# Block attention with decay followed by a two-layer network: the opening list laid out anew, decays spread by TensorE, zero fills in four, half products for w_in's second quarter

## The chip, the cores and the metric

The kernel runs on one core of one Trainium2 chip. The metric is the device time of one execution in microseconds (us). Three executions of the kernel before took 217.76, 217.8 and 218.54; their median is 217.8.

TensorE (PE in the profile, with its weight loads as PEld) multiplies, VectorE (DVE), ScalarE (ACT) and GpSimd (POOL) work on tiles, and SyncE (SP), ScalarE and GpSimd issue DMA transfers. Each engine works through its own queue in order; between the engines stand semaphore waits.

## What is computed

Inputs are q, k, v of shape (4 batches, 8 heads, 768 positions, 64), one decay lam per head, and the network's w_in (512 x 2048), w_out (2048 x 512) and alpha (2048).

```python
for b in range(nb):                      # blocks of 64 positions
    intra = einsum('bhic,bhjc->bhij', qb, kb) * Dmask      # lam ** (i - j) for j <= i
    intra = einsum('bhij,bhjd->bhid', intra, vb)
    inter = einsum('bhid,bhde->bhie', qb * lam_pow, kv_state)
    out[:, :, sl] = intra + inter
    kv_state = lam ** block * kv_state + einsum('bhsd,bhse->bhde', kb * rev_pow, vb)
x = out as (3072 positions, 512)
h = x @ w_in
g = maximum(h, 0) + alpha * minimum(h, 0)
return g @ w_out
```

## The kernel before

**Tiling.** Positions are taken 256 at a time. A chunk c (0 to 5) is one such stretch of two batches (bi 0 and 1): chunks 0 and 1 are the first stretch of the four batches, 2 and 3 the second, and so on. The attention of a chunk is split into four units: unit n has a chunk, a batch of it, and a half hh of the heads (four heads). Units 0 and 1 are batch 0's two halves in chunk 0, units 2 and 3 batch 1's, units 4 and 5 the first batch of chunk 1. When a chunk's four units are through, its outputs stand transposed in the tile xT, and the network runs over it.

**One unit's attention.** `cast` (L283) makes the fp16 tile qk of q or k on the engine that is named ("A" ScalarE, "V" VectorE, "G" GpSimd); `turn` (L303) transposes q and k on TensorE into one bank of PSUM, and `turned` (L324) copies that to SBUF as qkT. For units 1 to 3, q is taken from the fp16 tile qh, which a GpSimd DMA fills with a cast on the way. `scores` (L357) multiplies q and k into two banks s0 and s1, `masked` (L435) multiplies one of them with the decay mask on VectorE, `key_decayed` (L293) and `decayed` (L342) make the decayed keys (kdec) and queries (qdT). `cluster(old, new)` (L373) is TensorE's batch for two neighbouring units: the old unit's products with the state (L389) and with the masked scores (L409), and the new unit's scores, if they have not been made, and key-value products (L426). With `True` it uses the banks b0 and b1 (the name h_acc) and not the double bank acc. `state` (L461), `spread` (L490) and `out_of` (L440) then empty these banks: the state kept as KV or R, the state spread into the block-diagonal tile RD, and the output into xT. The tiles RD hold zeros off the diagonal, which `zeros` (L175) writes once at the start.

**The network.** `up(c, f, bi, slot)` (L506) makes 128 of the 2048 hidden columns of a chunk in a bank b0, b1 or b2: four matmuls of 512 columns for both batches (bi is None), or of 256 for one batch. `below` (L519) is ScalarE's part of the activation and `gate` (L524) VectorE's; both read the bank. `down` (L538) multiplies the gated tiles with w_out, `store` (L552) writes out. w_in comes in four quarters (`load_win`, L109), one for each four values of f: f 0 to 3 need the first quarter, 4 to 7 the second.

**Decays.** lam comes into all 128 partitions by one DMA (L62). `logs` (L197) takes its log on ScalarE; `mask_logs` (L212) makes the mask's exponents on VectorE, `mask_exp` (L226) the mask; `key_decay`, `query_decay` and `state_decay` (L230 to L240) the other powers.

**Order.** Up to L1100 the kernel is one list of steps written out by hand, which sets each engine's order; behind it loops weave the chunks. `fill(n, slot)` (L253) puts n matmuls of the tile spark into a bank: they keep TensorE at work and nobody reads them. `hold` (L83) writes one zero into a tile that a load will fill, so that SP's load waits for that point of VectorE's queue.

The list of before starts as follows (its lines 581 to 697, several steps to a line here):

```
light(); warm_up(); positions(); distances(); load("k", 0, 0, 0); logs(); load("q", 0, 0, 0); load16("q", 0, 1);
hold("k", 0, 1, 0); fill(40, 0); fill(1, 3); load16("q", 0, 0, 1); zeros(); fill(6, 3); fill(38, 0); mask_logs(1);
cast(0, "q", "A"); logs_by_pair(); key_decay(); identity(); load_alpha(); fill(14, 2); load("k", 0, 0, 1); load("k", 0, 1, 0);
cast(0, "k", "G"); mask_exp(1); turn(0); mask_logs(0); fill(3, 1); fill(12, 1); fill(7, 2); load("k", 0, 1, 1);
key_decayed(0, "V"); hold("k", 3, 0); load16("v", 0, 0, 0); load16("v", 0, 1); mask_exp(0); load16("v", 0, 0, 1);
query_decay(2, 0); load_win(0); key_decayed(1, "V"); load16("q", 1, 0); query_decay(1, 1); cast(1, "k", "V");
query_decay(0, 1); turn(1); turned(0, "V"); cluster(None, 0); hold("k", 1, 0); decayed(0, "G"); masked(0, 0); fill(8, 1);
query_decay(1, 0); cast(2, "k", "A"); state_decay(); query_decay(3, 1); turned(1, "V"); masked(0, 1); spread(0, 1, "A", True);
fill(4, 2); slopes(0); fill(2, 1); cast(3, "k", "A"); turn(2); turned(2, "V"); cluster(0, 1, True); masked(1, 1);
key_decayed(2, "G"); query_decay(2, 1); turn(3); fill(12, 2); state(0, 0); decayed(1, "G"); load_win(1); load16("v", 1, 0);
out_of(0, "A"); decayed(2, "G"); spread(1, 1, "A", True); masked(1, 0); state(1, 0); cluster(1, None); load_win(2);
key_decayed(3, "G"); fill(9, 0); fill(7, 1); cluster(None, 2); out_of(1, "A"); turned(3, "V"); spread(2, 1, "A", True);
masked(2, 0); up(0, 1, 0, 0); masked(2, 1); up(0, 2, 0, 2); below(0, 1, 0); below(0, 2, 0); load("k", 1, 0);
cluster(2, 3, True); gate(0, 1, 0); state(2, 0); load_win(3); gate(0, 2, 0); up(0, 0, 0, 2); cast(4, "k", "A"); ...
```

From `down(0, 0, 0, 2)` (L795) on, the two lists agree.

Of the kernel before, what the change touches and what calls it, by code (L numbers as in the profile page):

```python
# [11 lines left out]
def kernel(  # L12
# [16 lines left out]
    nc = tc.nc  # L29
# [105 lines left out]
    one = const.tile([128, 1], fp32, name="one")  # L135
    warm = const.tile([128, 1], fp32, name="warm")
    spark = const.tile([128, 128], fp16, name="spark")
    ident = const.tile([128, 128], fp16, name="ident")
    ident32 = const.tile([NF, NF], fp32, name="ident32")
    alpha_sb = const.tile([NF, 128], fp32, name="alpha_sb")  # L140
# [31 lines left out]
            )  # L172
        nc.gpsimd.iota(pos_i, pattern=[[1, 2], [0, 2], [2, 64]], base=1, channel_multiplier=0)

    def zeros():  # L175
        for t in RD.values():
            nc.vector.memset(t, 0.0)  # L177

    def light():
        nc.vector.memset(spark, 1.0)  # L180

    def warm_up():
        nc.vector.memset(one, 1.0)  # L183
# [28 lines left out]
    def mask_logs(hh, only=None):  # L212

        for hp in (2 * hh, 2 * hh + 1):
            for hl in range(2) if only is None else (only,):
                h = 2 * hp + hl
                nc.vector.scalar_tensor_tensor(  # L217
                    out=dmask[:, hl, hp],
                    in0=rel_f,
                    scalar=loglam[:, h : h + 1],  # L220
                    in1=future,
                    op0=ALU.mult,
                    op1=ALU.add,
                )
# [28 lines left out]
    def fill(n, slot=2):  # L253

        t = ps.tile([128, CH], fp32, tag="tk" if slot == 3 else f"b{slot}", name="op_fill")
        for _ in range(n):
            nc.tensor.matmul(t[:, 0:128], lhsT=spark, rhs=spark, start=True, stop=True)  # L257
# [321 lines left out]


    light()
    warm_up()
    positions()
    distances()
    load("k", 0, 0, 0)
    logs()
    load("q", 0, 0, 0)
    load16("q", 0, 1)
    hold("k", 0, 1, 0)
    fill(40, 0)  # L590
    fill(1, 3)
    load16("q", 0, 0, 1)
    zeros()
    fill(6, 3)
    fill(38, 0)
    mask_logs(1)
    cast(0, "q", "A")
    logs_by_pair()
    key_decay()
    identity()  # L600
    load_alpha()
    fill(14, 2)
    load("k", 0, 0, 1)
    load("k", 0, 1, 0)
    cast(0, "k", "G")
    mask_exp(1)
    turn(0)
    mask_logs(0)
    fill(3, 1)
    fill(12, 1)  # L610
    fill(7, 2)
    load("k", 0, 1, 1)
    key_decayed(0, "V")
    hold("k", 3, 0)
    load16("v", 0, 0, 0)
    load16("v", 0, 1)
    mask_exp(0)
    load16("v", 0, 0, 1)
    query_decay(2, 0)
    load_win(0)  # L620
    key_decayed(1, "V")
    load16("q", 1, 0)
    query_decay(1, 1)
    cast(1, "k", "V")
    query_decay(0, 1)
    turn(1)
    turned(0, "V")
    cluster(None, 0)
    hold("k", 1, 0)
    decayed(0, "G")  # L630
    masked(0, 0)
    fill(8, 1)
    query_decay(1, 0)
    cast(2, "k", "A")
    state_decay()
    query_decay(3, 1)
    turned(1, "V")
    masked(0, 1)
    spread(0, 1, "A", True)
    fill(4, 2)  # L640
    slopes(0)
    fill(2, 1)
    cast(3, "k", "A")
    turn(2)
    turned(2, "V")
    cluster(0, 1, True)
    masked(1, 1)
    key_decayed(2, "G")
    query_decay(2, 1)
    turn(3)  # L650
    fill(12, 2)
    state(0, 0)
    decayed(1, "G")
    load_win(1)
    load16("v", 1, 0)
    out_of(0, "A")
    decayed(2, "G")
    spread(1, 1, "A", True)
    masked(1, 0)
    state(1, 0)  # L660
    cluster(1, None)
    load_win(2)
    key_decayed(3, "G")
    fill(9, 0)
    fill(7, 1)
    cluster(None, 2)
    out_of(1, "A")
    turned(3, "V")
    spread(2, 1, "A", True)
    masked(2, 0)  # L670
    up(0, 1, 0, 0)
    masked(2, 1)
    up(0, 2, 0, 2)
    below(0, 1, 0)
    below(0, 2, 0)
    load("k", 1, 0)
    cluster(2, 3, True)
    gate(0, 1, 0)
    state(2, 0)
    load_win(3)  # L680
    gate(0, 2, 0)
    up(0, 0, 0, 2)
    cast(4, "k", "A")
    spread(3, 1, "A", True)
    masked(3, 0)
    decayed(3, "G")
    masked(3, 1)
    below(0, 0, 0)
    cluster(3, None)
    cast(4, "q", "G")  # L690
    state(3, 0)
    hold("k", 1, 1)
    out_of(2, "V")
    load("k", 1, 1)
    turn(4)
    load16("q", 1, 1)
    state(0, 1)
    out_of(3, "A")
    up(0, 3, 0, 0)
    up(0, 1, 1, 1)  # L700
    up(0, 2, 1, 2)
    turned(4, "A")
    below(0, 1, 1)
    decayed(4, "G")
    up(0, 5, None, 1)
    below(0, 2, 1)
    load16("v", 1, 1)
    cast(5, "k", "G")
    below(0, 3, 0)
    below(0, 5, None)  # L710
    up(0, 6, None, 2)
    gate(0, 0, 0)
    key_decayed(4, "V")
    below(0, 6, None)
    cluster(None, 4)
    up(0, 0, 1, 0)
    cast(5, "q", "G")
    gate(0, 1, 1)
    below(0, 0, 1)
    gate(0, 2, 1)  # L720
    key_decayed(5, "V")
    gate(0, 3, 0)
    turn(5)
    up(0, 3, 1, 1)
    up(0, 4, None, 2)
    gate(0, 5, None)
    gate(0, 6, None)
    load_wout(0)
    state(4, 0)
    gate(0, 0, 1)  # L730
    spread(4, 1, "G")
    up(0, 7, None, 0)
    below(0, 3, 1)
    below(0, 4, None)
    turned(5, "A")
    up(0, 8, None, 1)
    masked(4, 1)
    below(0, 8, None)
    gate(0, 3, 1)
    masked(4, 0)  # L740
    gate(0, 4, None)
    below(0, 7, None)
    up(0, 9, None, 2)
    state(3, 1)
    cluster(4, 5)
    below(0, 9, None)
    state(1, 1)
    cast(6, "q", "G")
    key_decayed(6, "G")
    hold("k", 2, 0)  # L750
    up(0, 11, None, 1)
    up(0, 12, None, 0)
    cast(6, "k", "A")
    gate(0, 8, None)
    turn(6)
    cast(7, "k", "G")
    hold("k", 2, 1)
    up(0, 10, None, 2)
    cast(7, "q", "A")
    out_of(4, "A")  # L760
    below(0, 12, None)
    gate(0, 7, None)
    up(0, 13, None, 0)
    gate(0, 9, None)
    load("k", 2, 0)
    below(0, 11, None)
    masked(5, 0)
    masked(5, 1)
    gate(0, 12, None)
    up(0, 14, None, 1)  # L770
    below(0, 10, None)
    load_wout(1)
    load("q", 2, 0)
    gate(0, 11, None)
    state(5, 0)
    spread(5, 1, "A")
    below(0, 13, None)
    below(0, 14, None)
    decayed(5, "G")
    turned(6, "V")  # L780
    cluster(5, None)
    load_wout(2)
    gate(0, 10, None)
    key_decayed(7, "G")
    cast(8, "k", "G")
    up(0, 15, None, 2)
    cluster(None, 6)
    out_of(5, "A")
    up(1, 1, 0, 1)
    below(0, 15, None)  # L790
    up(1, 2, 0, 0)
    gate(0, 13, None)
    gate(0, 14, None)
    turn(7)
    down(0, 0, 0, 2)  # L795
    spread(8, 0, "G")
    gate(0, 15, None)
# [400 lines left out]
```

## Time and profile before

| | |
|---|---|
| median of three executions | 217.8 us |
| the profiled execution | 217.74 us |
| its span, first to last instruction | 216.0 us |
| mean granted TensorE clock | 1.000 |
| matmuls in the span | 2224, of them 163 fills |

The profile is of one execution. A row of a timeline or a chain gives its start and its length in microseconds from the start of the span; a row of a group gives the busy time, the mean length of one in ns, and the idle time of the engine ahead of it. "L511" is line 511 of the kernel. A row "DMA to landing" gives the shortest, the middle and the longest time from a transfer's issue to its landing; for a single transfer the three are one number.

### The profile page before, as it was taken

The numbers are of one execution on the slowest core, as the hardware profiler recorded it, in microseconds if no ns is written. First come the engines' busy times: TensorE is split into PE (matmuls) and PEld (weight loads), VectorE is DVE, ScalarE is ACT, GpSimd is POOL, SyncE is SP. The second block draws the span as 40 slices with busy tenths as digits, with TensorE's granted clock in tenths as the row PEclk, the third lists the DMA queues.
The fourth block names the chain that finished last, engine by engine and source line by source line (L and its number), as shares of the span: only waits on it lengthen the run. The fifth ranks groups of instructions, "written<-read, shape, count | busy, mean of one in ns | idle before, by whom it ended". The sixth has DMA issues, their size and how long they took to land.

```text
span 216.0 us, 5454 instructions
## 1 busy us (share of the span) xinstructions
PE 208.6 (97%) x2224; PEld 114.7 (53%) x2224; DVE 136.9 (63%) x280; ACT 113.3 (52%) x222; POOL 88.9 (41%) x146
## 2 busy tenths in 40 slices
PE   8979899989999999999999999999999999999994
PEld 8958555544544555546554554554545444444442
DVE  3976999868597878888976646645746344435000
ACT  3777778841657645548745545545435534444120
POOL 8759547760088890193557266256221000000000
PEclk9999999999999999999999999999999999999999
DMA  5999999999999999987999242193011011110212
GB/s 131 218 195 223 203 210 251 214 167 190 314 273 154 253 157 195 180 178 191 196 279 177 40 100 72 25 100 84 16 49 49 5 49 49 49 43 8 97 49 99
DMA packets 63288, 29.85 MB, mean 138 GB/s; under 512 B 34192, under 2 KB 61088, under 8 KB 63264
## 3 DMA queue, kind: packets, MB, share of 16 engines
q1 hardware_dynamic: 38400, 15.01, 35.0%
q0 software_dynamic: 20368, 8.26, 31.9%
q10 hardware_dynamic: 4496, 6.24, 9.1%
q8 instruction: 17, 0.28, 0.6%
q14 instruction: 7, 0.06, 0.1%
HBM read 27.28 MB, written 6.29 MB: 155 GB/s over the span
## 4 chain that ended last, share of the span: by engine, by line
PE 89%; DVE 4%; ACT 3%; DMA 2%; issue 1%; DVEq 0%; ACTq 0%
PE h_ps L511 38%; PE o_ps L544 32%; PE o_ps L569 6%; PE s L365 4%; PE acc L409 3%; PE acc L389 2%; DMA lam_sb<-in_lam_dram 2%; PE acc L426 1%; DVE dmask L217 1%; DVE RD L177 1%; ACT m L522 1%; DVE g L534 1%; PE op_fill L257 1%; PE tp L318 1%; ACT RD L267 1%
## 5 line engine op out<-in xcount | busy, mean ns | idle before, releaser
L534 DVE SCALAR_TENSOR_TENSOR g<-m,oma,h_ps 128x512 f16<-128x512 f32 (+1 forms) x104 | 72.6, 704 | 50.0 <-ACT m L522 49.2
L511 PE MATMUL h_ps<-xT,w_in_sb 128*128 128x512 f16 (+1 forms) x416 | 95.7, 363 | 0.7 <-DVE g L534 0.7
L522 ACT ACTIVATE m<-h_ps 128x512 f32<-128x512 f32 (+1 forms) x104 | 57.9, 564 | 59.3 <-PE h_ps L511 56.9
L544 PE MATMUL o_ps<-w_out_sb,g 128*128 128x512 f16 x320 | 79.4, 379 | 0.7 <-DVE g L534 0.7
L511 PEld LDWEIGHTS <-w_in_sb 128*128 128x128 f16 x416 | 39.4, 98 | 42.3 <-issue 1.6
L544 PEld LDWEIGHTS <-g 128*128 128x128 f16 x320 | 30.5, 98 | 35.8 <-issue 1.0
L271 POOL COPY RD<-R 64x128 f16<-64x128 f16 x46 | 13.4, 290 | 52.0 <-DVE R L481 47.6
L438 DVE TENSOR_TENSOR sm<-s,dmask 128x512 f16<-128x512 f32 x48 | 31.9, 684 | 3.3 <-PE s L365 3.2
L267 ACT ACTIVATE o_sb<-o_ps 128x512 f32<-128x512 f32 (+1 forms) x24 | 14.2, 593 | 23.1 <-PE o_ps L544 12.5
L347 POOL TENSOR_TENSOR qdT<-qkT,qdecay 128x512 f16<-128x512 f16 (+1 forms) x21 | 20.5, 976 | 9.3 <-ACT qkT L267 4.4
L298 POOL TENSOR_TENSOR kdec<-kraw,kdecay 128x512 f16<-128x512 f32 x19 | 19.9, 1049 | 2.1 <-PE acc L426 1.9
L267 ACT ACTIVATE xT<-acc 128x512 f16<-128x512 f32 x19 | 11.3, 597 | 5.9 <-PE acc L426 4.5
L569 PE MATMUL o_ps<-w_out_sb,g 128*128 128x512 f16 (+2 forms) x80 | 14.0, 336 | 0.0
L257 PE MATMUL op_fill<-spark 128*128 128x128 f16 x163 | 12.5, 243 | 1.2 <-DVE one L183 1.1
L481 DVE SCALAR_TENSOR_TENSOR R<-R,rdecay,acc 128x64 f16<-128x64 f16 x48 | 11.2, 275 | 3.6 <-ACT xT L267 1.9
L257 PEld LDWEIGHTS <-spark 128*128 128x128 f16 x163 | 11.3, 111 | 1.7 <-DVE one L183 1.1
L271 POOL CAST qk<-kraw 128x512 f16<-128x512 f32 x14 | 9.0, 645 | 7.5 <-ACT RD L267 6.7
L102 POOL DMA_DIRECT2D vh<-in_v_dram x13 | 11.7, 904 | 0.0
L569 PEld LDWEIGHTS <-g 128*128 128x128 f16 x80 | 7.2, 98 | 6.9
L365 PE MATMUL s<-qkT 64*64 64x128 f16 x384 | 10.4, 222 | 0.0
L409 PE MATMUL acc<-sm,vh 64*64 64x128 f16 x352 | 9.0, 217 | 0.0
L389 PEld LDWEIGHTS <-RD 128*128 128x128 f16 x80 | 6.3, 98 | 4.8 <-ACT RD L267 0.4
(73 smaller groups left out, 126.3 us busy)
## 6 DMA issues: line engine op xcount, KB each, us to landing
kraw<-in_k_dram SPq DMA_DIRECT2D x10, 512.0 KB, 6.8
out_dram<-o_sb ACTq DMA_DIRECT2D x17, 256.0 KB, 3.0
qraw<-in_q_dram SPq DMA_DIRECT2D x8, 512.0 KB, 7.1
vh<-in_v_dram POOLq DMA_DIRECT2D x11, 256.0 KB, 7.4
w_in_sb<-in_moe_w_in_dram POOLq DMA_DIRECT2D x4, 512.0 KB, 9.5
w_out_sb<-in_moe_w_out_dram POOLq DMA_DIRECT2D x4, 512.0 KB, 8.7
out_dram<-o_sb ACTq DMA_DIRECT2D x12, 128.0 KB, 2.0
kraw<-in_k_dram SPq DMA_DIRECT2D x4, 256.0 KB, 5.3
```

The costliest lines, as they stand in the source:

```text
L257: nc.tensor.matmul(t[:, 0:128], lhsT=spark, rhs=spark, start=True, stop=True)
L267: nc.scalar.activation(out, in_, AF.Copy)
L271: nc.gpsimd.tensor_copy(out=out, in_=in_)
L298: engine(eng).tensor_tensor(out=kdec, in0=kr, in1=d.unsqueeze(3).to_broadcast([128, 2, 4, D]), op=ALU.mult)
L347: engine(eng).tensor_tensor(out=qdT[:, :, :, p], in0=t["qkT"][:, 0, :, :, p], in1=qdecay[:, hh, :, :, p], op=ALU.mult,)
L365: nc.tensor.matmul(s[hl][ds(a * 64, 64), hp, 1 - e, :].rearrange("p (e j) -> p e j", e=2), lhsT=t["qkT"][p, 1, e, hp, ds(a * 64, 64)], rhs ...
L438: nc.vector.tensor_tensor(out=t["sm"][hl], in0=t["s"][hl], in1=mask_of(hl, units[n][2]), op=ALU.mult)
L511: nc.tensor.matmul(h_ps[:, 0:n] if bi is None else h_ps[:, 0:n].rearrange("p (e j) -> p e j", e=2), lhsT=w_in_sb[:, gi, ts(f, 128)], rhs=x ...
L522: nc.scalar.activation(m[:, 0:n], HP[c, f, bi][:, 0:n], AF.Relu, scale=-1.0)
L534: nc.vector.scalar_tensor_tensor(out=g, in0=mv, scalar=oma[:, f : f + 1], in1=hv, op0=ALU.mult, op1=ALU.add)
L544: nc.tensor.matmul(O[c, t], lhsT=G[c, f][:, t // 2, t % 2, :], rhs=w_out_sb[:, f, :], start=(f == 0), stop=(f == NF - 1),)
L569: nc.tensor.matmul(o_ps[:, 0:n], lhsT=G[c, f][:, t // 2, t % 2, :], rhs=w_out_sb[:, f, ds(c0, n)], start=(f == 0), stop=(f == NF - 1),)
```

## The change

The functions that change, and those that are new:

```diff
-    lam_sb = const.tile([128, H], fp32, name="lam_sb")
+    lam_sb = const.tile([1, H], fp32, name="lam_sb")
     nc.scalar.dma_start(
         out=lam_sb,
-        in_=bass.AP(tensor=lam.tensor, offset=lam.offset, ap=[[0, 128]] + [list(p) for p in lam.ap]),
+        in_=bass.AP(tensor=lam.tensor, offset=lam.offset, ap=[[0, 1]] + [list(p) for p in lam.ap]),
     )
...
+    ones = const.tile([1, 128], fp32, name="ones")
...
-    def zeros():
-        for t in RD.values():
-            nc.vector.memset(t, 0.0)
+    LAM = {}
+
+    def zeros(b):
+        for hh in range(2):
+            nc.vector.memset(RD[b, hh], 0.0)
...
+    def all_ones():
+        nc.vector.memset(ones, 1.0)
...
+    def lam_all():
+
+        t = LAM[0] = ps.tile([128, CH], fp32, tag="tk", name="tp")
+        nc.tensor.matmul(t[:, 0:H], lhsT=ones, rhs=lam_sb, start=True, stop=True)
+
     def logs():
-        nc.vector.tensor_scalar(out=lamc, in0=lam_sb, scalar1=1e-18, scalar2=None, op0=ALU.max)
+        nc.vector.tensor_scalar(out=lamc, in0=LAM[0][:, 0:H], scalar1=1e-18, scalar2=None, op0=ALU.max)
```

lam now comes into one partition, and a matmul with a row of ones spreads it over 128. The rest of the diff is the list up to `down(0, 0, 0, 2)`. The new one starts so (lines 592 to 740 of the kernel after, several steps to a line here):

```
light(); all_ones(); fill(10, 2); zeros(2); load("q", 0, 0, 0); hold("k", 1, 0); positions(); distances(); identity();
lam_all(); warm_up(); load16("q", 0, 0, 1); load("k", 0, 0, 1); fill(13, 1); logs(); load("k", 0, 0, 0); key_decay();
fill(9, 3); cast(0, "k", "A"); mask_logs(0, 1); mask_logs(0, 0); logs_by_pair(); load16("v", 0, 0, 0); zeros(1);
cast(0, "q", "V"); cast(1, "k", "A"); load16("q", 0, 1); key_decayed(0, "V"); mask_exp(0); fill(12, 1); fill(3, 0);
fill(4, 2); query_decay(1, 1); turn(0); fill(4, 1); hold("k", 3, 0); load("k", 0, 1, 1); load16("v", 0, 0, 1);
load16("q", 1, 0); fill(13, 0); turned(0, "A"); load16("v", 0, 1); scores(0); mask_logs(1, 0); load_win(0);
mask_logs(1, 1); mask_exp(1); query_decay(0, 1); masked(0, 0); load("k", 0, 1, 0); turn(1); fill(20, 2); zeros(0);
load_win(1); load("k", 1, 0); load_alpha(); turned(1, "A"); query_decay(2, 1); cast(2, "k", "A"); cluster(None, 0);
cast(3, "k", "A"); masked(0, 1); load16("v", 1, 0); key_decayed(1, "V"); decayed(0, "V"); load_win(2); query_decay(3, 1);
hold("k", 0, 1, 0); fill(1, 1); fill(4, 0); spread(0, 1, "V", True); cast(4, "k", "A"); turn(2); fill(7, 0); scores(1);
cluster(0, 1, True); state(0, 0); turned(2, "V"); key_decayed(2, "G"); masked(1, 1); turn(3); state_decay(); masked(1, 0);
spread(1, 1, "A", True); state(1, 0); decayed(1, "G"); turned(3, "V"); load_win(3); decayed(2, "G"); scores(2);
cluster(1, None); fill(18, 2); out_of(1, "A"); cluster(None, 2); masked(2, 1); cast(5, "k", "A"); masked(2, 0);
out_of(0, "V"); slopes(2); spread(2, 1, "A", True); key_decayed(3, "G"); scores(3); cast(4, "q", "G"); turn(4);
cluster(2, 3, True); hold("k", 2, 0); decayed(3, "G"); query_decay(1, 0); masked(3, 0); state(2, 0); cast(5, "q", "A");
state(3, 0); load16("q", 1, 1); load16("v", 1, 1); masked(3, 1); out_of(2, "A"); turned(4, "V"); zeros(3);
spread(3, 1, "A", True); up(0, 0, 0, 2); up(0, 1, 0, 1); below(0, 0, 0); below(0, 1, 0); fill(2, 3); load_wout(0);
key_decayed(4, "G"); cluster(3, None); up(0, 2, 0, 0); out_of(3, "A"); up(0, 0, 1, 2); gate(0, 0, 0); key_decayed(5, "G");
gate(0, 1, 0); below(0, 2, 0); up(0, 3, 0, 1); query_decay(2, 0); up(0, 4, 1, 0); below(0, 0, 1); cluster(None, 4);
below(0, 4, 1); gate(0, 2, 0); up(0, 4, 0, 2); below(0, 3, 0); decayed(4, "V"); hold("k", 2, 1); hold("k", 1, 1);
turn(5); gate(0, 0, 1); state(4, 0); ...
```

Of the products of chunk 0, those with f 4 to 7 (the second quarter) are now made by batch too, so that f 0 to 7 are halves; before, f 0 to 3 were. Fourteen of the sixteen halves stand ahead of the first whole product, f 11, and the second batch's halves of f 2 and 3 behind it, among the whole ones. The fills are 120, where they were 163. `scores` of units 0 to 3 are steps of their own ahead of their clusters. zeros(0) to zeros(3) write the two tiles of one batch each. SP's first six loads are, in order, q(0,0,0), k(0,0,1), k(0,0,0), k(0,1,1), k(0,1,0) and the whole k(1,0). GpSimd makes the identity ahead of its transfers, and issues the transfers of q and v and the first two quarters of w_in in a row, with v(1,0) and the third quarter right behind. `hold("k", 0, 1, 0)` stood ahead of its load and now stands behind it, so it sets one loaded element of that tile to zero between cast(2, "k") and key_decayed(2).

More of the change, by code (lines that the diff above doesn't have):

```diff
@@ L581 @@
     light()
-    warm_up()
+    all_ones()
+    fill(10, 2)
+    zeros(2)
+    load("q", 0, 0, 0)
+    hold("k", 1, 0)
     positions()
     distances()
-    load("k", 0, 0, 0)
-    logs()
-    load("q", 0, 0, 0)
-    load16("q", 0, 1)
-    hold("k", 0, 1, 0)
[L590 to L603, printed above, removed]
@@ L680 @@
-    load_win(3)
-    gate(0, 2, 0)
[L682 to L691, printed above, removed]
-    hold("k", 1, 1)
-    out_of(2, "V")
-    load("k", 1, 1)
-    turn(4)
-    load16("q", 1, 1)
+    identity()
+    lam_all()
+    warm_up()
+    load16("q", 0, 0, 1)
+    load("k", 0, 0, 1)
+    fill(13, 1)
+    logs()
+    load("k", 0, 0, 0)
+    key_decay()
@@ new lines @@
+    fill(9, 3)
+    cast(0, "k", "A")
+    mask_logs(0, 1)
+    mask_logs(0, 0)
+    logs_by_pair()
+    load16("v", 0, 0, 0)
+    zeros(1)
+    cast(0, "q", "V")
+    cast(1, "k", "A")
+    load16("q", 0, 1)
+    key_decayed(0, "V")
+    mask_exp(0)
+    fill(12, 1)
+    fill(3, 0)
+    fill(4, 2)
+    query_decay(1, 1)
+    turn(0)
+    fill(4, 1)
+    hold("k", 3, 0)
+    load("k", 0, 1, 1)
+    load16("v", 0, 0, 1)
+    load16("q", 1, 0)
+    fill(13, 0)
+    turned(0, "A")
+    load16("v", 0, 1)
@@ new lines @@
+    scores(0)
+    mask_logs(1, 0)
+    load_win(0)
+    mask_logs(1, 1)
+    mask_exp(1)
+    query_decay(0, 1)
+    masked(0, 0)
+    load("k", 0, 1, 0)
+    turn(1)
+    fill(20, 2)
+    zeros(0)
+    load_win(1)
+    load("k", 1, 0)
+    load_alpha()
+    turned(1, "A")
+    query_decay(2, 1)
+    cast(2, "k", "A")
+    cluster(None, 0)
+    cast(3, "k", "A")
+    masked(0, 1)
+    load16("v", 1, 0)
+    key_decayed(1, "V")
+    decayed(0, "V")
+    load_win(2)
+    query_decay(3, 1)
+    hold("k", 0, 1, 0)
@@ new lines @@
+    fill(1, 1)
+    fill(4, 0)
+    spread(0, 1, "V", True)
+    cast(4, "k", "A")
+    turn(2)
+    fill(7, 0)
+    scores(1)
+    cluster(0, 1, True)
+    state(0, 0)
+    turned(2, "V")
+    key_decayed(2, "G")
+    masked(1, 1)
+    turn(3)
+    state_decay()
+    masked(1, 0)
+    spread(1, 1, "A", True)
+    state(1, 0)
+    decayed(1, "G")
+    turned(3, "V")
+    load_win(3)
+    decayed(2, "G")
+    scores(2)
+    cluster(1, None)
+    fill(18, 2)
+    out_of(1, "A")
+    cluster(None, 2)
@@ new lines @@
+    masked(2, 1)
+    cast(5, "k", "A")
+    masked(2, 0)
+    out_of(0, "V")
+    slopes(2)
+    spread(2, 1, "A", True)
+    key_decayed(3, "G")
+    scores(3)
+    cast(4, "q", "G")
+    turn(4)
+    cluster(2, 3, True)
+    hold("k", 2, 0)
+    decayed(3, "G")
+    query_decay(1, 0)
+    masked(3, 0)
+    state(2, 0)
+    cast(5, "q", "A")
+    state(3, 0)
+    load16("q", 1, 1)
+    load16("v", 1, 1)
+    masked(3, 1)
+    out_of(2, "A")
+    turned(4, "V")
+    zeros(3)
+    spread(3, 1, "A", True)
@@ new lines @@
+    hold("k", 2, 1)
+    hold("k", 1, 1)
+    turn(5)
+    gate(0, 0, 1)
+    state(4, 0)
+    load_wout(1)
+    gate(0, 4, 1)
+    up(0, 1, 1, 0)
+    below(0, 4, 0)
+    load("k", 1, 1)
+    up(0, 5, 1, 1)
+    gate(0, 3, 0)
+    gate(0, 4, 0)
+    below(0, 5, 1)
+    up(0, 5, 0, 2)
+    spread(4, 1, "G")
+    cast(6, "q", "G")
+    state(1, 1)
+    up(0, 6, 1, 1)
+    masked(4, 0)
+    cast(6, "k", "G")
+    up(0, 7, 1, 2)
+    gate(0, 5, 1)
+    below(0, 5, 0)
+    turned(5, "A")
+    below(0, 1, 1)
@@ L773 @@
[L773 to L782, printed above, removed]
-    gate(0, 10, None)
[L784 to L794, printed above, removed]
+    gate(0, 6, 0)
+    below(0, 12, None)
```

223 lines of the change are left out of this document (80 added, 143 removed).

## The prediction

> **What bounds the kernel now.** I read the page's busy times first, then the granted clock and busy time in three stretches, then TensorE's waits, then the chain of waits over the first 30 us, and last the issue and landing of single transfers.
>
> ```profile
> span 216.0 us, 5454 instructions
> PE 208.6 (97%) x2224; PEld 114.7 (53%) x2224; DVE 136.9 (63%) x280; ACT 113.3 (52%) x222; POOL 88.9 (41%) x146
> 0.00:19.69 19.69, 17.08 (x340) 15.37 (x341) 13.26 (x41) 11.84 (x28) 14.71 (x28) 1.00 1.20 191
> 19.69:42.27 22.58, 21.79 (x331) 13.52 (x322) 20.90 (x43) 18.00 (x41) 15.05 (x24) 1.00 1.32 219
> 42.27:216.00 173.73, 169.78 (x1567) 85.83 (x1564) 102.73 (x198) 83.46 (x154) 59.13 (x96) 1.00 0.64 122
> 0.00:19.69 19.69, 12.53 (x163) 1.00 1.20 191
> PE o_ps L544 <- DVE g L534: 0.7, 1, 0.7
> PE h_ps L511 <- DVE g L534: 0.7, 2, 0.5
> ```
>
> The columns of the stretches are length, busy time of PE, PEld, DVE, ACT and POOL, then the granted clock, DMA share and GB/s; the fourth stretch row counts PE's op_fill alone. TensorE sets the time: from 19.69 us (first product with w_in) it is nearly always busy. Before 19.69 it is busy for 17.08 us, but 12.53 of them are the 163 fills, which compute nothing: only 4.55 us of needed work is done there. All the change touches lies before the first `down` (42.27 us), since the lists agree behind it. The end therefore moves by three things: when the first product starts, how much needed work TensorE has done by then, and its waits afterwards. Those are 1.4 us (0.7 + 0.7): two of h_ps, and one of o_ps at the seam.
>
> Why does the first product start so late? The chain says:
>
> ```profile
> 0.74 3.76 DMA lam_sb<-in_lam_dram
> 4.74 0.27 DVE RD L177
> 6.93 1.19 DVE dmask L217 x4
> 8.60 1.41 DVE dmask L217 x4
> 10.00 0.60 DVE kdec L298 x2
> 11.55 0.60 DVE qkT L269
> 12.93 0.35 PE s L365 x16
> 19.76 0.98 PE h_ps L511 x8
> ```
>
> lam lands at 4.5; then everything stands in VectorE's queue: eight zero fills (the first at 4.74, 0.27 each), both halves of the mask's logs, key decays and the copy qkT, until scores(0) at 12.93. The products follow 6.8 us later.
>
> **The change part by part.**
>
> *The front.* VectorE's fills, the second mask half, one cast and the first two qkT copies leave the path before scores(0). What takes their place is lam, the third SP load and ScalarE's queue.
>
> ```profile
> out_dram<-o_sb SPq DMA_DIRECT2D x1, 64.0 KB, 1.6
> DMA to landing us min/median/max: 4.6/4.6/4.6
> 6.33 1.28 ACT L232 ACT_TABLE_LOAD   x1
> 7.62 0.49 ACT L232 ACTIVATE kdecay<-loglam,rev_f 128x8 f32<-128x8 f32 x2
> 5.68 0.63 ACT L267 ACTIVATE qk<-qraw 128x512 f16<-128x512 f32 x1 [0.74 <-DMA qraw<-in_q_dram]
> 8.16 0.84 ACT L228 ACTIVATE dmask<-dmask 128x768 f32<-128x768 f32 x1
> 10.79 1.26 ACT L240 ACTIVATE qdecay<-pos_f,llp 128x128 f32<-128x128 f32 x4
> 24.00 1.02 ACT L267 ACTIVATE qkT<-tp 128x1024 f16<-128x1024 f16 x1
> ```
>
> The second row is the landing of before's third SP load (issued at 1.79), so the new third load, k(0,0,0), is due at 6.4. For lam in one partition no row exists; between the shortest landing shown (1.6 us) and its own of before (3.76) it lands at 2.3 to 4.5. Behind it stand the tiny spreading matmul and two small operations (I allow 0.8 with hops), a table load 1.28 and kdecay 0.49: 4.9 to 7.1. I take 6.4, the load's own time, for any lam up to 3.8. Then ScalarE: casts 0 and 1 (0.63 each), mask_exp 0.84, one query decay 0.38 (1.26 for four overlapped), turned(0) 1.02: scores(0) at 10.0, or 10.7 with a late lam, against 12.93. The ends are 2.2 and 2.9 us earlier. zeros(2), zeros(1), zeros(0) and zeros(3) (two fills each, 0.54) now lie where VectorE waits: ahead of lam, ahead of the loads, between masked(0,0) and masked(0,1), and behind turned(4). If that cover goes they cost their 0.54 each.
>
> *Needed work before the first product.* The new list puts the whole of units 0 to 3 but the last cluster, and turn(4), ahead of `up(0,0,0)`. Before, these came behind the first product:
>
> ```profile
> 20.85 0.58 PE s L365 x16
> 21.82 0.19 PE h_acc L426 x14
> 22.61 0.28 PE acc L389 x2
> 22.89 0.53 PE acc L409 x16
> 28.77 0.45 PE tp L318 x8
> ```
>
> scores(3), the two products of unit 2 (one in each slot, 0.11 to 0.28 and 0.35 to 0.53 by what surrounds them), the key-value product 0.12 and turn(4) 0.45: 1.25 to 1.75 us. I take **-1.5**. It holds if the attention is through when the weights land. In before cluster(2,3) ended (second row) 9.1 us behind the start of scores(0) (22.0 less 12.93), so now at 19.1 to 19.8.
>
> *The first product* waits for w_in's first quarter. It is issued in both kernels near 8 us, but now behind more loads.
>
> ```profile
> 7.82 0.77 POOL L110 DMA_DIRECT2D w_in_sb<-in_moe_w_in_dram  x1
> DMA to landing us min/median/max: 9.4/9.4/9.4
> DMA to landing us min/median/max: 11.5/11.5/11.5
> 4.00:31.35 27.35, 25.16 (x480) 19.74 (x478) 23.11 (x58) 19.21 (x49) 18.83 (x29) 1.00 1.39 215
> ```
>
> The landings are of the first quarter (17.2) and of the fourth, the slowest of the four. Counting what lands in SBUF, 2,688 KB are issued up to and with the first quarter in before; now 3,456 KB (SP: five halves of 256 and k(1,0) with 512; POOL: 1,152 of q and v, 512 of w_in), 768 KB more. The DMA engines are full there (share 1.39, the queues' packets overlapping), at 215 GB/s: 3.7 us more, 20.9. The other end: POOL starts its transfers after the identity, about 2.9, six of some 0.88 each stand ahead, so it issues at 8.2; with the fourth quarter's 11.5 it lands at 19.7. I take 20.2, **+0.5** against 19.69 (0 to +1.2). The later quarters are covered: the second now follows directly, 512 KB or 2.4 us behind (22.6), and five half products at 0.49 and two clusters stand before its first use near 23.7; the third, with v(1,0), is due near 26.3, its first use near 30; the fourth is issued behind POOL's kdec(2) and qdT(1), near 15.3, ahead of its first use near 31 by more than the longest landing.
>
> *Four more pairs of half products* (0.98 for two halves in the chain, so TensorE loses nothing: 0.44 to 0.49 each against 0.86 for a whole) but more for the others:
>
> ```profile
> L534 DVE SCALAR_TENSOR_TENSOR g<-m,oma,h_ps 128x512 f16<-128x512 f32 x12 | 8.6, 744 | 1.4 <-ACT m L522 1.3
> L534 DVE SCALAR_TENSOR_TENSOR g<-m,oma,h_ps 128x256 f16<-128x256 f32 x10 | 4.7, 476 | 0.7 <-ACT m L522 0.6
> L438 DVE TENSOR_TENSOR sm<-s,dmask 128x512 f16<-128x512 f32 x48 | 31.9, 684 | 3.3 <-PE s L365 3.2
> 17.55 0.45 ACT L476 ACTIVATE KV<-h_acc 128x128 f32<-128x128 f32 x2
> 16.43 0.66 ACT L267 ACTIVATE xT<-h_acc 128x256 f16<-128x256 f32 x2 [1.00 <-PE h_acc L426]
> ```
>
> Two halves cost VectorE 0.21 more than a whole, and a half (0.476) as long as its product takes. Fourteen halves now stand in a row: 6.7 us, and with two masks (0.684 each), states and a decay I put VectorE at 9.3 us there, against TensorE's 8.0 with unit 4's attention; three banks (1.35) absorb that, or not: 0 to 1.3. The second product needs bank 1, which cluster(2,3) fills and ScalarE empties (KV 0.45, xT 0.66) while the first runs 0.49: a wait of 0.6. New waits: 0.4 to 1.9, and I take **+0.7**; the old 1.4 vanish, since at the seam `up(0,15)` and its gate come well ahead: **-1.4**.
>
> *Waits and queues.* cast(4,"k") waits on ScalarE for k(1,0), with KV(0), rdecay and RD(0,1) behind it; hold("k",0,1,0), now behind its load, makes VectorE wait for k(0,1,0) and cast(2), with spread(0) and turned(2) behind it. ScalarE reaches them near 13 to 14; SP issues both by 3.3; its 1,792 KB at 215 GB/s take 8.5 us from about 3, so k(1,0) lands at 11.5, or at 14.5 with POOL's first four transfers (640 KB) in between. No cost taken; each microsecond past 14 costs up to one. [...]
>
> Sum: -1.5 + 0.5 - 1.4 + 0.7 = -1.7. The profiled execution took 217.74 (1.74 around its span), so 216.0; the median of 217.8 lies 0.06 above it.
>
> **The rivals.**
>
> *The clock stays at half.*
>
> ```profile
> 1.05 4.40 PEld L257 LDWEIGHTS <-spark 128*128 128x128 f16 x42 [1.05 <-DVE one L183]
> 5.65 3.22 PEld L257 LDWEIGHTS <-spark 128*128 128x128 f16 x57 [0.20 <-issue]
> ```
>
> The fills run at 105 ns each (4.40/42) for 4.4 us and at 56 (3.22/57) from then on, so the array starts at half speed and speeds up after steady work. Now TensorE has ten fills (to 2.1) and then idles until lam, so the step may come later. [...]
>
> *The change doesn't do what it says: the front is faster but hidden.* If v(0,1), due only 2.4 us or so ahead of the first w_in quarter, or ScalarE's longer queue holds unit 2, TensorE fills as before and the 1.5 falls away: 217.4. For it: TensorE takes its list in order.
>
> *The first w_in quarter comes late: slower.* Each microsecond past 20.2 is one at the end, for only two fills stand behind it. From 21.9 nothing is won, from 23.0 it is slower by over 0.5%. For it: three more loads in a full DMA stretch, and v, q and k(1,0) all ahead; against: the same bytes at 215 GB/s give 20.9 at worst. At 23.3 it would be 219.1.
>
> *No transfer binds.* With landings of 9.4 us as before (17.6) the front itself, 19.1, sets the first product (-0.6 instead of +0.5) and the waits stay at 0.4: 214.6.
>
> **How the numbers follow.** Forecast 0.48 (own range 215.0 to 217.2), no transfer binds 0.16, hidden front 0.12, clock 0.10, late weights 0.14. Within 0.5% (1.1 us, about what can be told from no change here) lies 216.7 to 218.9. Faster: 0.42 of the forecast and 0.16; same: 0.06, 0.20 of hidden front and clock; the rest slower. That is 0.58, 0.26 and 0.16. The range 214.2 to 218.8 leaves out the worse part of the late weights and a little below.
>
> **What would show it.** Right: scores(0) near 10; the chain's first 10 us on ScalarE; the first h_ps near 20.2, ended by w_in's landing at 19.7 to 20.9; needed work before it near 6 us; no o_ps wait at the seam; first `down` near 41.3. Wrong: fills at 105 ns past 9 us; ScalarE idle on k(1,0); VectorE idle at hold; h_ps waiting for over 2 us in all.

## The result and the profile after

The changed kernel takes **220.95 us** (median of 4 runs, 220.53 to 220.99) against 217.9 us before (4 runs, 217.76 to 218.54): 1.0139 times, 95% interval 1.0127 to 1.0151. It is slower, where 216.0 was forecast with a range to 218.8. The profiled execution took 220.93, of which the span is 219.0. A few executions fall into a slower state; two of those below did (223.35 with the later w_out, 220.03 in the second set of the 512-column kernel), and they are left out of medians, ranges and ratios.

First the page, then the same three stretches as were shown of before (up to the first product, up to the first `down`, the rest; the columns are length, busy time of PE, PEld, DVE, ACT and POOL, then clock, DMA share, GB/s):

```profile
span 219.0 us, 5413 instructions
PE 208.6 (95%) x2199; PEld 114.4 (52%) x2199; DVE 138.8 (63%) x286; ACT 113.7 (52%) x225; POOL 89.7 (41%) x147
0.00:22.23 22.23, 18.06 (x355) 15.07 (x355) 17.23 (x50) 15.04 (x32) 19.39 (x34) 1.00 1.26 197
22.23:46.11 23.88, 20.70 (x285) 13.70 (x281) 17.59 (x39) 15.27 (x40) 9.68 (x18) 1.00 1.18 199
46.11:219.00 172.89, 169.79 (x1567) 85.67 (x1564) 103.97 (x198) 83.37 (x154) 60.65 (x97) 1.00 0.64 120
```

TensorE is busy for as long as before (208.6 us), so all 3.0 us of longer span are waits. They stand where the change was made: the first product comes 2.54 later (22.23 against 19.69), the stretch from there to the first `down` is 1.30 longer (23.88 against 22.58), the rest is 0.84 shorter (172.89 against 173.73; the 0.74 at the seam is gone, as forecast). What TensorE waited for up to there, by the view of waits (total, times, longest):

```profile
PE h_acc L437 <- issue: 1.8, 1, 1.8
PE tp L329 <- POOL qk L282: 1.0, 1, 1.0
...
PE h_ps L522 <- DVE g L545: 0.8, 2, 0.6
PE acc L400 <- POOL RD L282: 0.7, 1, 0.7
PE h_ps L522 <- ACT xT L278: 0.5, 1, 0.5
```

Two of these were in no part of the forecast: 1.8 for "issue", time in which the engine waits for nothing that the profile shows, and the pair 1.0 and 0.7 for POOL. The timeline of TensorE shows the first in its place (start, length, line, operation; a wait in brackets):

```profile
19.10 0.62 PE L329 MATMUL tp<-ident,qk 128*128 128x128 f16 x8
19.55 0.28 PE L400 MATMUL h_acc<-qdT,RD 128*128 128x128 f16 x2
19.76 0.42 PE L420 MATMUL h_acc<-sm,vh 64*64 64x128 f16 x16
20.01 0.26 PE L437 MATMUL h_acc<-vh,kdec 64*64 64x64 f16 x11
22.06 0.24 PE L437 MATMUL h_acc<-vh,kdec 64*64 64x64 f16 x5 [1.79 <-issue]
22.23 0.61 PE L522 MATMUL h_ps<-xT,w_in_sb 128*128 128x256 f16 x4
23.38 0.60 PE L522 MATMUL h_ps<-xT,w_in_sb 128*128 128x256 f16 x4 [0.54 <-ACT xT L278]
```

TensorE stops inside `cluster(2,3)`, after eleven of sixteen matmuls of one product, whose operands were there: v(0,1) had landed at 17.2, kdec(3) was done at 17.4. Nothing that the profile shows releases it. In the DMA records a packet of the queue named "instruction", 16 KB, starts 0.5 us before the stop, at 19.77. The second pair is in the chain of waits (start, length, what):

```profile
25.95 0.42 DVE qdT L358
26.36 0.04 DVE kraw L85
26.46 12.43 DMA kraw<-in_k_dram
39.02 0.49 POOL qk L282
39.58 0.76 POOL w_out_sb L116
...
42.13 0.24 POOL RD L282
```

This is k(1,1). Its `hold` stands in VectorE's queue behind the first gates and runs at 26.36, its load is issued at 26.46 and takes 12.4 us, beside two parts of w_out that GpSimd had issued at 20.35 and 23.12. GpSimd waits for it with its cast; turn(6) waits 0.99 for that cast, and cluster(5,None) 0.75 for the spread that is queued behind it.

### The profile page after: what moved, and what is told of

It reads as the page before. It is cut to its first block, busy times and chain, and to the rows that moved or that the text cites. A ratio compares the mean times of both kernels' runs of the same rounds, so it can differ in the third digit from the quotient of the medians.

```text
span 219.0 us, 5413 instructions
## 1 busy us (share of the span) xinstructions
PE 208.6 (95%) x2199; PEld 114.4 (52%) x2199; DVE 138.8 (63%) x286; ACT 113.7 (52%) x225; POOL 89.7 (41%) x147
## 4 chain that ended last, share of the span: by engine, by line
PE 83%; DMA 10%; POOL 3%; issue 2%; ACT 1%; DVE 0%; POOLq 0%; DVEq 0%; SPq 0%
PE h_ps L522 33%; PE o_ps L555 32%; PE o_ps L580 6%; DMA kraw<-in_k_dram 6%; DMA qh<-in_q_dram 4%; PE s L376 3%; PE acc L420 2%; PE acc L400 2%; PE acc L437 1%; PE op_fill L268 1%; POOL qk L282 1%; PE tp L329 1%; ACT xT L278 1%; PE tp L325 0%; POOL qh L102 0%
## 5 line engine op out<-in xcount | busy, mean ns | idle before, releaser
L533 ACT ACTIVATE m<-h_ps 128x512 f32<-128x512 f32 (+1 forms) x108 | 58.6, 550 | 61.9 <-PE h_ps L522 60.5
L522 PEld LDWEIGHTS <-w_in_sb 128*128 128x128 f16 x432 | 41.0, 98 | 42.7 <-issue 2.8
L282 POOL COPY RD<-R 64x128 f16<-64x128 f16 x46 | 13.4, 291 | 49.9 <-DVE R L492 45.2
L309 POOL TENSOR_TENSOR kdec<-kraw,kdecay 128x512 f16<-128x512 f32 x21 | 21.9, 1052 | 1.8 <-PE acc L437 1.4
L358 POOL TENSOR_TENSOR qdT<-qkT,qdecay 128x512 f16<-128x512 f16 (+1 forms) x19 | 19.1, 1006 | 1.7 <-ACT qkT L278 0.7
L282 POOL CAST qk<-kraw 128x512 f16<-128x512 f32 x13 | 8.4, 652 | 13.9 <-DMA kraw<-in_k_dram 13.5
L268 PE MATMUL op_fill<-spark 128*128 128x128 f16 x120 | 10.7, 259 | 1.1 <-DVE spark L183 1.1
L268 PEld LDWEIGHTS <-spark 128*128 128x128 f16 x120 | 9.3, 119 | 1.4 <-DVE spark L183 1.1
```

The costliest lines, as they stand in the source:

```text
L282: nc.gpsimd.tensor_copy(out=out, in_=in_)
L309: engine(eng).tensor_tensor(out=kdec, in0=kr, in1=d.unsqueeze(3).to_broadcast([128, 2, 4, D]), op=ALU.mult)
L358: engine(eng).tensor_tensor(out=qdT[:, :, :, p], in0=t["qkT"][:, 0, :, :, p], in1=qdecay[:, hh, :, :, p], op=ALU.mult,)
L522: nc.tensor.matmul(h_ps[:, 0:n] if bi is None else h_ps[:, 0:n].rearrange("p (e j) -> p e j", e=2), lhsT=w_in_sb[:, gi, ts(f, 128)], rhs=x ...
L533: nc.scalar.activation(m[:, 0:n], HP[c, f, bi][:, 0:n], AF.Relu, scale=-1.0)
```

## The experiments

**Does TensorE run out of instructions?** Two runs of the changed kernel, with fewer TensorE instructions for the same busy time, and with more. The first makes the fills 512 columns wide and a quarter in number, the second puts 16 more narrow fills into a hole behind turn(0).

```diff
-    spark = const.tile([128, 128], fp16, name="spark")
+    spark = const.tile([128, CH], fp16, name="spark")
...
-        for _ in range(n):
-            nc.tensor.matmul(t[:, 0:128], lhsT=spark, rhs=spark, start=True, stop=True)
+        for w in [CH] * (n // 4) + [128] * (n % 4):
+            nc.tensor.matmul(t[:, 0:w], lhsT=spark[:, 0:128], rhs=spark[:, 0:w], start=True, stop=True)
```

> Changed kernel with one edit: the fills compute 512 columns instead of 128 and are a quarter in number (120 become 39), so TensorE is kept as busy by fewer instructions. Theory A (TensorE ran out of loaded instructions): it stops for 1.79 us inside the key-value product of unit 3, after eleven of its sixteen matmuls, where no semaphore stands; a 16 KB packet of the instruction queue starts at 19.77 and TensorE goes on at 22.06. With 162 fewer TensorE instructions (81 fills of two each) ahead of that point the next packet is needed only among the half products, which use instructions far more slowly: the wait is gone, first h_ps near 20.5 instead of 22.3, time 219.2 against 220.95. Rival B (that matmul waits for data, a transfer or another engine): the wait stays at the same matmul, time 220.9.

```diff
-    fill(13, 0)
+    fill(29, 0)
     turned(0, "A")
```

> Changed kernel with 16 more narrow fills in the hole behind turn(0) (8.90 to 9.77, where TensorE was idle). Theory A (instructions run out after a fixed count): 32 more TensorE instructions ahead, so the wait of about 1.8 us moves 16 matmuls forward, out of the key-value product into the product acc<-sm,vh of unit 2 ahead of it, with some five of its sixteen matmuls behind the wait; time as of the changed kernel, 220.9. Rival B (the twelfth matmul of the key-value product waits for data): the wait stays behind the eleventh matmul of the key-value product, time 220.9.

The 512-column fills gave **217.23** (10 runs, 216.31 to 218.7), 0.9962 of before (0.9936 to 0.9989): 3.7 us less than the changed kernel and 2.0 less than theory A expected, since the two waits for POOL were gone from the profiled run as well. The fills are 42 instead of 120, and not 39. The other kernel took 219.44 in its one run, less than expected, since its wait came out at 1.06 instead of 1.8 and that of turn(6) for POOL at 0.2 instead of 1.0. First TensorE's timeline with the 16 more fills:

```profile
19.43 0.28 PE L400 MATMUL h_acc<-qdT,RD 128*128 128x128 f16 x2
19.64 0.36 PE L420 MATMUL h_acc<-sm,vh 64*64 64x128 f16 x11
21.06 0.30 PE L420 MATMUL h_acc<-sm,vh 64*64 64x128 f16 x5 [1.06 <-issue]
21.14 0.34 PE L437 MATMUL h_acc<-vh,kdec 64*64 64x64 f16 x16
```

and then with the 512-column fills:

```profile
18.05 0.25 PE L376 MATMUL s<-qkT 64*64 64x128 f16 x3
18.51 0.41 PE L376 MATMUL s<-qkT 64*64 64x128 f16 x13 [0.21 <-issue]
...
19.76 0.29 PE L437 MATMUL h_acc<-vh,kdec 64*64 64x64 f16 x16
```

Sixteen more matmuls ahead, and the wait stands sixteen matmuls earlier, in another product (eleven of the key-value product and five of the one before it). With 78 matmuls fewer ahead (118 fills become 40), cluster(2,3) runs through, and a wait of 0.21 stands after three matmuls of scores(3). That place is 13 + 8 + 2 + 16 + 11 = 50 matmuls ahead of the old one, so TensorE stops 128 matmuls earlier by count: behind its 222nd matmul instead of its 350th. Each has a weight load of its own: 256 instructions, in a packet of 16 KB. The wait belongs to the count, not to any data. It is shorter here, but not gone: six of the kernels with wide fills below show 0.3 to 0.7 at the same count.

Read from the trace's records, the times around this count (us; "passed" is when TensorE went past the count one block, 128 matmuls, ahead, "reached" when it came to the end of the block that it had; early_key, late_wout and wide_late are kernels of the experiments further down):

```
kernel        passed  packet starts  reached  goes on
before        15.9    18.12          20.6     20.8
after         16.0    19.77          20.3     22.06
more_fills    15.2    18.76          20.0     21.06
early_key     15.8    19.37          20.1     21.81
late_wout     17.3    20.24          21.7     22.64
wide_fills    13.2    16.24          18.3     18.51
wide_fills    18.5    22.29          24.7     24.7
wide_late     13.0    16.36          18.1     18.72
```

Wherever TensorE was there first, it goes on 2.3 to 2.4 us behind the start of the packet, and the packet starts 2.9 to 3.8 us behind the passing of the count. So a block takes 5.3 to 6.1 us from passing to going on, and the changed kernel wants 128 matmuls in 4.3. The kernel before used the same block in 4.7, but its packet started 2.2 behind the passing, which with 2.3 more makes 20.4: just in time. The packets ahead of it and behind it start 2.5 us (8.6 to 11.07) and 3.6 us (20.8 to 24.42) after such a passing, so 2.2 is no fixed property of that kernel; by the same estimate, with 3.6 it would have stopped too. What makes a packet start later wasn't tried apart; the DMA share in the first stretch is 1.26 in the changed kernel against 1.20.

Over the whole span the page has 17 packets of that queue, 0.28 MB, for 2199 matmuls and as many weight loads, which is 17.2 times 256. The one that was late in the changed kernel cost it 1.79 us.

**Are the wide fills worth something in themselves?** The same edit in the kernel before.

> The kernel before with 512-column fills, a quarter in number; nothing else. Theory A (the wide fills help only by removing TensorE's wait for instructions, and the kernel before has no such wait): no change, 217.9. Rival E (fewer, wider fills are worth something in themselves): faster by 1 us or more.

217.74 against 217.74 (ratio 0.9999, 0.9989 to 1.0008). They are worth nothing in a kernel without such a wait, so the 3.7 us are put down to the wait and what follows from it.

**Why is k(1,1) late?** Moved earlier, alone and with the wide fills:

```diff
-    hold("k", 2, 0)
+    hold("k", 1, 1)
+    load("k", 1, 1)
...
-    hold("k", 1, 1)
+    hold("k", 2, 0)
...
-    load("k", 1, 1)
```

> Changed kernel with k(1,1) loaded earlier: its hold takes the place of that of k(2,0) in VectorE's queue (18.99 instead of 26.3) and the load stands right behind it. Theory C (k(1,1), issued at 26.46 behind two parts of w_out, lands at 38.9 and stops turn(6) for 0.99 and, through GpSimd, which waits 8.0 for it with a spread queued behind, cluster(5,None) for 0.75): both waits vanish, time 219.2 against 220.95. Rival D (the loads only change places): now k(1,1) stands ahead of parts of w_in and w_out, a wait of h_ps for w_in or of o_ps for w_out takes their place, time 220.5 to 221.5.

> Both edits together: 512-column fills and the early load of k(1,1). If both waits are independent the gains add: 220.95 - 1.8 - 1.7 = 217.4, about the kernel before. If the loads only follow TensorE's pace (rival D), 218.7 to 219.2.

220.78 (four runs, 218.45 to 221.31; 1.0108, 1.0046 to 1.017) and 218.26 (1.0003, 0.9975 to 1.0032): alone no gain clear of the spread, and together 1.0 us worse than the wide fills alone. The two waits for POOL are gone in both profiled runs. In the second kernel the price came up elsewhere, as rival D had it in kind, though neither at w_in nor at w_out:

```profile
PE acc L437 <- DMA vh<-in_v_dram: 1.3, 1, 1.3
```

v(1,0), issued at 9.7 in both, lands 17.0 us later, against 13.4 in the 512-column kernel. In the first kernel two other things stood in the profiled run: VectorE's four state steps took 2.41 us, against 0.86 in the changed kernel, for a cause that the profile doesn't show (its chain of waits has them as below), and TensorE's clock fell (last section). The run of 218.45 alone kept a mean clock of 1.000, the other three had 0.992; so what the early load is worth without these disturbances stays open.

```profile
33.37 2.41 DVE R L492 x4
```

So the other way: leave k(1,1) where it is and issue w_out later.

```diff
-    load_wout(0)
...
-    load_wout(1)
...
     spread(4, 1, "G")
+    load_wout(0)
...
     cast(6, "k", "G")
+    load_wout(1)
```

> The changed kernel with narrow fills and its wait for instructions, but the first two parts of w_out issued later: behind the spread of unit 4 and behind the cast of unit 6's keys in GpSimd's queue, near where the kernel before has them. Theory C (k(1,1) comes late because 1 MB of w_out, issued at 20.4 and 23.1, is in the DMA engines beside it): k(1,1) lands well before 38.9, the waits of 0.99 and 0.75 vanish while that of 1.8 stays, 219.2 against 220.95. Rival L (k(1,1) is late only because it is issued at 26.5; the landing follows from the start of its queue, not from w_out): the two waits stay, 220.9.

219.45 (three runs, 219.1 to 219.61; 1.007, 1.0046 to 1.0093), 1.5 below the changed kernel. The first product was even later in the profiled run (22.82: the wait for instructions was 0.97, but TensorE also waited 1.15 for a transfer of q, and its mean clock was 0.991), k(1,1) was issued later too, at 27.05, and yet GpSimd has it at 33.92:

```profile
33.92 0.61 POOL L282 CAST qk<-kraw 128x512 f16<-128x512 f32 x1 [2.85 <-DMA kraw<-in_k_dram]
34.48 1.50 POOL L116 DMA_DIRECT2D w_out_sb<-in_moe_w_out_dram  x2
```

and no wait of TensorE for POOL is left. Theory C holds: with 1 MB of w_out issued ahead of it k(1,1) took 12.4 us, without at most 6.9 (33.92 less 27.05).

**Both edits together**, beside the 512-column kernel once more on the same chip:

> The two causes removed together, nothing else: 512-column fills and the first two parts of w_out issued later. Theory C: in the 512-column kernel k(1,1) lands in time in the profiled run (216.31) but its runs reach 218.7, as kernels with a first product only 0.8 later wait 0.5 to 0.7 for the spread behind it; with the later w_out the median falls from 217.2 to 216.4 to 216.8. Rival N (the spread of the runs has another source, such as the start of the front): the median stays at 217.2.

> The 512-column kernel once more, on the same chip as the one above, so that the two can be compared directly: 217.2 by its earlier runs; by theory C above the kernel with the later w_out by 0.4 to 0.8, by rival N equal to it.

**216.68** (10 runs, 216.52 to 217.38; 0.995 of before, 0.9933 to 0.9968) and 216.96 (11 runs, 216.43 to 218.06; 0.9962, 0.9942 to 0.9982). The gain between them, 0.3, is below the 0.4 to 0.8 that were expected, and the intervals overlap, so rival N isn't excluded by the medians. The spread is narrower: nine of the 21 runs of the 512-column kernel, in both sets, lie above 217.38, the slowest with the later w_out. In the second one's profiled run (218.06) the first product came at 20.5, and the wait for the spread was back:

```profile
PE acc L400 <- POOL RD L282: 0.7, 1, 0.7
```

In its earlier profile (216.31), with the first product at 20.0, it was absent. So the late k(1,1) is a second cause, but one that a late first product sets off, by the first cause or otherwise (no wait for instructions shows in the run of 218.06): its load is issued at TensorE's pace.

**The new waits at the products.** Four edits of the 512-column kernel. First `cluster(3,None)` moved ahead of `up(0,0,0,2)`:

> The 512-column kernel with cluster(3,None) moved from behind the first two products to directly ahead of the first. There the second product waits 0.56 for the copies of cluster(2,3) that empty bank 1. Theory F (0.46 us of TensorE work put into that hole): the wait falls to about 0.1 and the end comes 0.4 to 0.5 earlier, 216.8 against 217.2. Rival G (ScalarE copies and VectorE masks of unit 3 are late, so the product of unit 3 waits in the same place): no change.

219.53 (1.0091, 1.0063 to 1.0119), a clear miss: rival G named ScalarE's copies, but not what they would cost. TensorE's wait was 1.53:

```profile
20.24 0.29 PE L437 MATMUL h_acc<-vh,kdec 64*64 64x64 f16 x16
22.06 0.29 PE L400 MATMUL acc<-qdT,RD 128*128 128x128 f16 x2 [1.53 <-POOL kdec L309]
```

while ScalarE worked off what cluster(2,3) had left:

```profile
20.59 0.45 ACT L487 ACTIVATE KV<-h_acc 128x128 f32<-128x128 f32 x2
20.92 0.67 ACT L278 ACTIVATE xT<-h_acc 128x256 f16<-128x256 f32 x2
21.45 0.56 ACT L278 ACTIVATE RD<-h_acc 64x128 f16<-64x128 f32 x2
```

The product of unit 3 reads the state RD that spread(3) copies out of that same cluster, last of six copies, at 22.01. (The profile names POOL, whose kdec ended at about that time; the operands say RD.) The two products that stood ahead of it had covered just that. The two waits for POOL came back too (0.7 each).

Then f 4 to 7 made whole, as `up(0, 4, None, 0)`, `up(0, 5, None, 1)`, `up(0, 6, None, 0)`, `up(0, 7, None, 1)` where their first halves stood:

> The 512-column kernel with the second quarter (f 4 to 7) made whole again, each where its first half stood. Theory H (the four more pairs of halves overload VectorE, and TensorE waits 0.61 + 0.12 + 0.17 for gates): VectorE has 4 x 0.21 less to do, these waits fall to 0.2 or less, the first down comes 0.6 to 0.9 earlier, 216.5. Rival I (the waits come from the masks and state steps in VectorE's queue, or the whole products need three banks longer): the waits stay at 0.7 to 1.0, no change.

217.25 (0.9971, 0.9954 to 0.9988): no change. Its waits, 0.56 behind the first product and 0.38 and 0.61 later, come to as much as those of the halves (0.56, 0.61, 0.12, 0.17). The four pairs of halves cost nothing that these runs can tell.

Then `out_of(2, "V")`, with banks 0 and 1 changed between the second and the third product, alone and with the later w_out:

> The 512-column kernel with the bank of the second product emptied sooner: out_of(2) copied by VectorE (as in the kernel before) beside ScalarE's copies of KV, and the second and third product change banks (0 and 1). Theory F2 (the second product waits 0.56 only for ScalarE's queue of four copies): the wait falls to 0.1 or less and the end comes 0.4 to 0.5 earlier, 216.7 against 217.2. Rival M (VectorE's copy delays turned(4) and the gates behind it by 0.75): the gain is given back at the gates, 217.2 or more.

> All three edits: 512-column fills, the emptied bank, the later w_out. In the 512-column kernel k(1,1) stopped nothing in the profiled run, so by theory C the later w_out adds little there but makes it safe against later starts: 216.5 to 216.8, under both the kernel before (217.9) and the 512-column kernel (217.2). If w_out then comes late for the first down, o_ps waits appear and the time is 217.5 or more.

219.26 (1.0066, 1.0042 to 1.0091) and 218.26 (1.0021, 1.0009 to 1.0033): both worse than without the edit, a miss for F2. The second product's wait grew to 0.89:

```profile
PE h_ps L522 <- ACT RD L278: 0.9, 1, 0.9
```

Bank 0 holds what spread(3) reads, and VectorE's copy did not run beside ScalarE's but behind it (KV from 20.89, xT from 21.20), with the spread behind both (21.66). A wait of 0.45 for a gate and, in the first of the two, 0.5 for the spread of unit 4 came on top. The kernel's bank 1 was the one free first.

Last, lam broadcast again by its transfer, without the spreading matmul:

> The 512-column kernel with lam again broadcast to 128 partitions by its transfer, and no spreading matmul. Theory J (the earlier decays shorten the front): lam lands near 4.5 instead of 2.2, scores(0) moves from 9.6 to about 10.7, cluster(2,3) ends up to 1.0 later than 20.05, and the end moves by as much: 217.7 to 218.2. Rival K (ScalarE's casts and the landing of k(0,0,0) at 6.6 set scores(0), not lam): no change, 217.2.

219.2 (1.007, 1.0045 to 1.0096), 2.0 above the 512-column kernel. TensorE's timeline:

```profile
8.23 0.89 PE L329 MATMUL tp<-ident,qk 128*128 128x128 f16 x8 [2.41 <-ACT qk L278]
10.68 0.42 PE L376 MATMUL s<-qkT 64*64 64x128 f16 x16 [0.64 <-ACT qkT L278]
```

scores(0) at 10.68, as expected, and the first product at 21.35, 1.37 later; 0.3 of that is a longer wait for instructions (0.52 against 0.21). With it the wait of 0.74 for the spread behind k(1,1) came back, which makes 2.1. The front is not hidden.

## Why the prediction was wrong

*The front* was right: scores(0) at 9.77 (10.0 forecast), behind ScalarE's turned(0). The chain that leads to the first product doesn't run over it, though, but over GpSimd's issues and the transfer of q for units 2 and 3, up to 13.58; so the sign of a chain on ScalarE in the first 10 us failed.

```profile
9.77 0.42 PE L376 MATMUL s<-qkT 64*64 64x128 f16 x16 [0.87 <-ACT qkT L278]
4.91 8.67 DMA qh<-in_q_dram
```

*The first quarter of w_in* was right too: issued at 8.28, it landed 11.5 us later, at 19.77, at the lower end of 19.7 to 20.9, and the later quarters at 22.4, 26.3 and 28.9 stopped nothing. The rival of late weights had the sign right, but nothing waited for weights. The attention was last, as in the rival where no transfer binds; but it would have ended at 20.4, and not at that rival's 19.1. The forecast had carried over the 9.1 us from scores(0) to its end; even without the stop they were 10.6 (9.77 to 20.4), and why was not tried apart.

*The first product at 20.2 was the step that failed.* cluster(2,3) began at 19.55 and would have ended at 20.4; the forecast took for granted that TensorE can run as fast as data and engines let it. By packing 128 matmuls into 4.3 us it came to the end of its instructions 1.8 us before the next block was there. No row on which the forecast rests tells this beforehand; the instruction queue's packets do, and the count of TensorE's instructions from block to block. Of the 4.7 us between the forecast span and the measured one, 2.0 lie here and 1.7 at k(1,1); new waits and less work moved make up the rest.

*The other rivals.* The clock: the step came later, as that rival had it (fills start 107 ns apart up to 7.0, where in before those from 5.7 on were at 56), but the fills behind turn(0) start 56 ns apart from 7.79 on, ahead of the 9 us that the forecast names as the sign. The hidden front: refuted by the kernel with lam's broadcast, which was 2.0 slower.

*Needed work ahead of the first product* (-1.5): what lies between it and the first `down` fell from 21.79 to 20.70, -1.1; 0.28 of the 20.70 are two fills, so the needed work fell by 1.4. The sign for it failed even so: ahead of the first product TensorE was busy for 7.7 us besides the fills (18.06 less 10.40), not near 6.

*New waits* (+0.7, 0.4 to 1.9): 0.54 + 0.61 + 0.12 + 0.17 = 1.44 of h_ps, mis-sized but inside; the 0.54 was forecast as 0.6. That VectorE's four more pairs cause the rest is not borne out: with whole products these waits were as long.

*k(1,1)* wasn't in the sum, though the change put two parts of w_out ahead of it and its hold behind three gates: 0.99 + 0.75 = 1.74. The part on queues weighed k(1,0) and the hold of k(0,1), which cost nothing, and not the next load of the same kind.

In the kernel of 216.68 the waits for POOL are gone and the wait for instructions is down to 0.6 (last row), so the forecast's terms can be read one by one:

```profile
0.00:20.20 20.20, 17.05 (x277) 9.66 (x278) 16.20 (x47) 15.05 (x32) 17.83 (x32) 1.00 1.24 201
20.20:42.04 21.84, 20.37 (x291) 13.89 (x281) 18.72 (x43) 15.16 (x40) 11.59 (x20) 1.00 1.32 220
42.04:214.70 172.66, 169.62 (x1567) 85.71 (x1564) 103.00 (x198) 83.31 (x154) 59.67 (x97) 1.00 0.63 122
PE s L376 <- issue: 0.6, 1, 0.6
```

First product +0.51 (+0.5 forecast), work 21.79 to 20.37, -1.4 (-1.5; without the two fills -1.7), waits in the second stretch 1.47 (21.84 less 20.37) against 0.79, +0.7 where the two waits of h_ps that fall away and the new ones were forecast at 0.0, the rest -1.07 (-0.74). That is -1.3 of span, against -1.7. The agreement at the first product is luck: w_in's first quarter landed at 19.0 there, and the attention, with those 0.6 in it, set the 20.2.

## What to carry to other kernels

Where a change packs many small matmuls closely (here 128 in 4.3 us, at a DMA share of 1.26), count TensorE's instructions between the packets of its instruction queue: the 120 narrow fills used up instructions that TensorE needed next, and 42, 26 of them wide, kept it busy for as long (10.6 us against 10.7). Before a load that is late by several us is moved forward, look at what is beside it: moving bulk weights back cost nothing here, while with the load moved forward another, v(1,0), landed 3.6 us later. A delay of the first product is more than itself where later loads are issued from queues that follow it: 1.37 became 2.0, and a wait shorter by 1.6 became 3.7.

## What was not expected of the hardware

In the changed kernel and its variants a block of TensorE's instructions was there 5.3 to 6.1 us after TensorE had passed the count one block ahead, with a DMA share of 1.26 in the changed kernel's first stretch; in the kernel before it was there after 4.9 at most (15.9 to 20.8).

Behind nearly the same hole TensorE's clock fell in one run and stayed in another. In the profiled run with the early key TensorE was idle for 1.68 us up to 21.81, and its granted clock was 0.50 from 22.60 for 3.41 us; the changed kernel, with a hole of 1.79 in the same place, kept 1.00. Two stretches of each (columns as above):

```profile
23.00:24.00 1.00, 0.87 (x5) 0.61 (x5) 0.06 (x1) 0.87 (x4) 0.92 (x2) 0.50 1.20 218
24.00:25.00 1.00, 1.00 (x21) 0.70 (x19) 0.83 (x2) 0.38 (x1) 0.00 (x0) 0.50 1.20 212
```

```profile
23.00:24.00 1.00, 0.62 (x8) 0.57 (x7) 0.00 (x0) 0.96 (x5) 0.91 (x2) 1.00 1.26 212
24.00:25.00 1.00, 1.00 (x25) 0.76 (x23) 0.81 (x2) 0.83 (x3) 0.00 (x0) 1.00 1.24 201
```

The first two are of the early key, the others of the changed kernel. With the later w_out and narrow fills the profiled run has a mean clock of 0.991. What makes the clock fall is not shown.

Three of the four executions of the changed kernel have a mean clock of 0.990 to 0.992, which fits one such stretch at half speed (half of 3.41 in 219 is 0.8%, an estimate), and took 220.53 to 220.99; the profiled one has 1.000 and took 220.93. So the clock is not what made the changed kernel slow.
